# First weights of the next sequence ahead of this one's sums with v, and weights stored whole through DRAM

## The chip, the cores and the metric

One core of a Trainium2 chip. The kernel takes attention inputs and the weights of a channel-mix layer from DRAM and writes one output to DRAM. The metric is the device time of one execution in microseconds; the times given are the median of three runs. TensorE is called PE, VectorE DVE, ScalarE ACT, SyncE SP.

## What is computed

Eight sequences of 576 tokens, 8 heads of 64 channels. 32 packed queries p attend to k and v; then each q attends to the 32 packed values, which serve as keys and as values. The result, 512 channels for each token, goes through a channel mix with a shift by one token. All of it is float32.

```python
def sm_attn(qq, kk, vv):
    s = scale * np.matmul(qq, kk.transpose(0, 1, 3, 2))
    a = np.exp(s - np.max(s, axis=-1, keepdims=True))
    a = a / (np.sum(a, axis=-1, keepdims=True) + 1e-09)
    return np.matmul(a, vv)
p_packed = sm_attn(p, k, v)
out = sm_attn(q, p_packed, p_packed)
...
x_prev = np.concatenate([np.zeros((B, 1, D), dtype=np.float32), x[:, :-1, :]], axis=1)
xk = mu_k * x + (1.0 - mu_k) * x_prev
xr = mu_r * x + (1.0 - mu_r) * x_prev
k = np.maximum(xk @ w_k, 0.0)
v = k * k @ w_v
r = 1.0 / (1.0 + np.exp(-(xr @ w_r)))
return (r * v).astype(np.float32)
```

## The kernel before

The channel mix runs over 9 blocks of 512 tokens. A product of two float32 matrices is made as three matmuls of halves, a high part and the rest (`wk_h`, `wk_l`, and so on), so every 128x512 piece of a product with 128 channels takes three matmuls. Blocks 0 to 2 are done one after the other (`gates`, `keys`, `values`: 48, 96 and 96 matmuls each). Blocks 3 to 8 are done in three pairs, where a pair's products use seven products of sums and differences instead of eight (`products_of`, matmuls at line 1430). They need sums of the weights' blocks, which `chain_of_sums` makes on DVE, splits and sends to DRAM, and differences of the mixed inputs, which `chain_of` makes; the chain of the first pair's keys is called A. Between block 2 and the first pair stand the gates of blocks 3 and 4 (`turned_gates`, lines 1586 to 1588): 96 matmuls, called the seam here with the last of the attention that must be done by then.

Attention of a sequence b goes through these steps. `front`: scores of the packed queries (line 600), weights of both halves of the heads (`weights_of`: maximum at line 667, exponential at line 673). From sequence 2 on the weights are turned by a trip through DRAM (`weights_moved`: a transpose in 32x32 blocks on DVE at line 716, a write `away<-blocks`, four reads `aT<-away` per half). Then, still in `front`, the sums with v (line 622), a division and one transpose on PE. `scores`: second scores (line 749). `back`: softmax over 32 on DVE (lines 765 to 784), a transpose (line 788), products with the packed values (line 796, two bursts for each sequence), copied by ACT to `xt` and stored as `xd`. Scores and products take two slots (`pa`) of two PSUM banks each.

Sequence 0 is split in halves of the heads (`first_side`); its steps stand ahead of the first channel-mix matmul, with dummy matmuls (`spare`) that the planner puts where it reckons PE to be waiting. The weights w_r, w_k, w_v are loaded as pieces of 128x512 (`st`), decoded and split (`convert`, lines 348 to 364).

The order of all of it is made by a planner at build time (class `Flow`): each step is a generator that asks for an engine, a slot or an event, and of those ready the planner takes the one that can start first, with ties by rank. Most numbers at the head of the kernel are ranks. All loads and stores but a few go through SP's queue, in the order in which the planner issues them. Every engine works in order, so the order is fixed once built, and what waits holds up all that is behind it on its engine.

Of the kernel before, what the change touches and what calls it, by code (L numbers as in the profile page):

```python
# [8 lines left out]
F32 = mybir.dt.float32  # L9
# [8 lines left out]
class Flow:  # L18
# [13 lines left out]
    URGENT = 17.786  # L32
# [158 lines left out]
def attn_pack_channel_mix(ctx: ExitStack, tc: tile.TileContext, q, k, v, p, p_first, mu_first, mu_by_channel, w_k, w_v, w_r, out):  # L191
    nc = tc.nc
    B, NPR, P, S = q.shape
    D = P // 2
# [19 lines left out]
    FIRST = 6.558, 12.87, 19.531, 3.995  # L214
    RANK_1, RANK_MIX, RANK_KEYS, RANK_R, RANK_W, RANK_W2, RANK_V, LOADS_1, RANK_SQ, RANK_REST, HOLD_V, HOLD_S = 27.755, 14.838, 10.91, 19.059, 8.25, 30, 30, 23.598, 1.16, -7.23, 0.413, 0.153
    RANK_LATE1 = 0.221
    RANK_LATE2 = 2.192
    RANK_LATE3 = 4.603
    RANK_LATE4 = 0.433
    RANK_LATE5 = 6.623  # L220
    RANK_LATE6 = 7.657
    RANK_LATE13 = 27.996
    RANK_LATE12 = 15.041
# [37 lines left out]
    def reached():  # L261
# [12 lines left out]
    BUFS = dict(kq=8, vt=2, xin=0, pt=1, a0=1, a1=1, aT=1, pm=2, e=4, a2=1, xt=5, tmp=4, xk=NC, sq=NF, sig=4,  # L274
                pa=2, both=1, m=4, n=4, staged=4, ex=3, pair=0, ring=0, store=4, twin=0)
# [11 lines left out]
    RANK_B, RANK_TURN, RANK_BACK, RANK_OUT, RANK_L = 0.2, 1.444, 0.355, 8, 6.94  # L287
    CASTS = 3
    RANK_SUMS = dict(k=28.195, v=34.766, r=31.397)
    CHAINS = dict(A=(1.411, 44.286), B=(11.166, 24.664), RB=(5.884, 12.059), C=(14.13, 14.447), RC=(0.2, 0.2))  # L290
# [9 lines left out]
    for tag, n, size in (  # L300
        ("xk", NC, 2 * TB), ("sq", NF, 2 * TB), ("tmp", 4, WP), ("sig", 4, DM), ("kq", 8, S),
        ("a2", 1, S), ("ex", 3, TB), ("e", 4, S), ("aT", 1, 5 * P), ("vt", 2, NPR * 5 * D),
    ):
        for j in range(n):
            sb.tile([P, size], F32, name=tag, tag=f"{tag}{j}")
    for j, size in enumerate((S, 5 * P)):
        sb.tile([P, size], F32, name="a", tag=f"a{j}")
# [19 lines left out]
    def convert(w, hi, lo, c, o, n, event, first=None):  # L327
# [36 lines left out]
        nc.vector.tensor_tensor(lo[:, c, o:o + n], m.bitcast(F32), hi[:, c, o:o + n].bitcast(F32), op=ALU.subtract)  # L364
        flow.give("tmp", sm)
        flow.set(event)
# [3 lines left out]
    def rank(b, n=0):  # L370

        return (10 if b == 0 else RANK_1 if b == 1 else RANK_B) + 0.1 * (2 * b + n)

    def lrank(b):
        return LOADS_1 if b == 1 else rank(b) if b < 2 else RANK_L + 0.2 * b
# [16 lines left out]

    def loads(b):
        flow.spawn(packed(b), lrank(b) - 0.03)
        for pr in range(NPR):
            flow.spawn(turned(k, "kT", b, pr), lrank(b) - 0.02)
        for h in range(2):
            flow.spawn(values_of(b, h), lrank(b) - 0.01)
        for pr in range(NPR):
            flow.spawn(turned(q, "qT", b, pr), lrank(b))  # L400
        yield from flow.wait(*(("qT", b, pr) for pr in range(NPR)))
# [33 lines left out]
    def first_side(h):  # L435
# [32 lines left out]
        flow.give("a1" if h else "aT", sT)  # L468
# [121 lines left out]

    def front(b):

        yield from flow.wait(("pt", b), *(("kT", b, pr) for pr in range(NPR)))
        slots = yield from two_slots()
# [14 lines left out]
        for h in range(2):  # L609
            flow.spawn(weights_of(b, h, slots[h], s1[h], sm), rank(b) + 0.01 * h)  # L610

        yield from flow.wait(("aT", b, 0))
        slot = yield from flow.take("pa")
# [3 lines left out]
        both = [(*vts.pop((b, h)), *aTs.pop((b, h))) for h in range(2)]  # L617

# [15 lines left out]
        for h, (sv, _, sT, _) in enumerate(both):  # L634
            flow.give("a1" if h else "aT", sT)
            flow.give("vt", sv)
# [6 lines left out]
        sp = yield from flow.take("pm")  # L643
# [8 lines left out]
        nc.tensor.transpose(pT[:, :P], pm.rearrange("p a b -> p (a b)"), ident)  # L652
        ppT = sb.tile([P, P], F32, name="ppT", tag="ppT")
# [8 lines left out]
    def weights_of(b, h, slot, s1, sm):  # L662
# [7 lines left out]
        sa = yield from flow.take(f"a{h}")  # L670
        a = tile_([P, S], F32, "a", h)
# [6 lines left out]
        if b >= MOVED:  # L678
            yield from weights_moved(b, h, sa, a)
            return  # L680
# [7 lines left out]
        if h:  # L688

            sT, aT = sa, tile_([P, 5, P], F32, "a", 1, "aT")  # L690
        else:
            flow.give("a0", sa)
            sT = yield from flow.take("aT")
            aT = tile_([P, 5, P], F32, "aT", sT)
# [15 lines left out]
    def weights_moved(b, h, sa, a):  # L710

        space = "e"
        se = yield from flow.take(space)
# [3 lines left out]
        if h:  # L717

            sT, aT = sa, tile_([P, NPR, 5, NP], F32, "a", 1, "aT")
        else:  # L720
            flow.give("a0", sa)
            sT = yield from flow.take("aT")
            aT = tile_([P, NPR, 5, NP], F32, "aT", sT)
        away = dram.tile([P, NTB, NP], F32, name="away", tag=f"away{h}")
# [15 lines left out]
    def scores(b, sp, pm, ppT, left):  # L740

        yield from flow.wait(*(("qT", b, pr) for pr in range(NPR)))
        slots = yield from two_slots()
# [1088 lines left out]
```

## Time and profile before

| | |
|---|---|
| median of 3 runs | 561.11 us (558.93 to 563.09) |
| profiled execution | 559.48 us |
| its span, first to last instruction | 557.5 us |
| mean granted clock of PE | 0.993 |
| PE busy | 543.8 us, 98% of the span |
| DVE busy | 463.4 us, 83% |
| ACT busy | 388.3 us, 70% |
| transfers | 119.69 MB, 215 GB/s over the span |

The profile shows one execution. A matmul's row gives its start and its duration; matmuls overlap, so the distance between starts is shorter than a duration. What stands in brackets behind a row of the timeline is the idle time before it and what ended it. A window's row gives, after its length, the busy time and the instructions of each engine, then the granted clock, the share of time in which the 16 transfer engines were busy, and GB/s.

### The profile page before, as it was taken

What the parts mean: (1) busy time and instruction counts of PE and PEld (TensorE: products, weight loads), DVE (VectorE), ACT (ScalarE), POOL (GpSimd) and SP (SyncE); (2) the same over time, 40 slices, a digit from 0 to 9 for tenths busy, and PEclk for the clock granted to TensorE, in tenths of its full rate; (3) what the DMA queues carried; (4) which work ended last, traced back from release to release, by engine and by line L of the source; (5) the groups of instructions that cost most, each with busy time, mean ns of one, the idle gap of its engine ahead of it and who ended that gap; (6) DMA issues with size and microseconds to landing.
All of it is one profiled execution on the core that took longest, in us unless ns stands there. A gap on an engine that the chain in (4) does not pass through costs nothing.

```text
span 557.5 us, 10174 instructions
## 1 busy us (share of the span) xinstructions
PE 543.8 (98%) x3571; PEld 421.6 (76%) x3571; DVE 463.4 (83%) x888; ACT 388.3 (70%) x745; POOL 2.8 (1%) x27
## 2 busy tenths in 40 slices
PE   8999999999999999996999999999999999999997
PEld 7956677777776777774888788888888888878885
DVE  1785888989889979999885897957999894799863
ACT  3689897558556777656878775489886748897550
POOL 1000000000000000000000000000000000000000
PEclk9999999999999999997999999999999999999999
DMA  8986956589798998766567814819462681934242
GB/s 278 406 312 245 314 179 210 200 299 320 254 309 249 350 314 268 213 200 200 185 213 229 260 51 148 266 35 287 129 218 78 210 265 33 284 122 152 66 143 94
DMA packets 86930, 119.69 MB, mean 215 GB/s; under 512 B 9440, under 2 KB 58080, under 8 KB 86880
## 3 DMA queue, kind: packets, MB, share of 16 engines
q1 hardware_dynamic: 85600, 117.67, 64.6%
q10 hardware_dynamic: 1280, 1.38, 0.7%
q8 instruction: 28, 0.46, 0.3%
q14 instruction: 22, 0.18, 0.1%
HBM read 87.29 MB, written 31.73 MB: 213 GB/s over the span
## 4 chain that ended last, share of the span: by engine, by line
PE 71%; DVE 11%; DMA 9%; ACT 7%; issue 1%; SPq 0%; DVEq 0%; ACTq 0%
PE ph L1430 44%; PE ph L999 4%; PE ph L1000 4%; PE ph L1001 4%; DMA xin<-xd 3%; PE pa L796 1%; PE pr L1586 1%; PE pr L1587 1%; PE pvo L1099 1%; DMA kT<-in_k 1%; PE pr L1588 1%; PE pr L1070 1%; PE pa L622 1%; DMA qT<-in_q 1%; PE pvo L1100 1%
## 5 line engine op out<-in xcount | busy, mean ns | idle before, releaser
L1430 PE MATMUL ph<-vT,ring 128*128 128x512 f32 x270 | 66.1, 392 | 0.0
L1430 PEld LDWEIGHTS ph<-vT,ring 128*128 128x128 f32 x270 | 50.7, 188 | 11.1
L1430 PE MATMUL ph<-vB,wv_h 128*128 128x512 f32 x140 | 43.7, 394 | 0.8 <-DMA wv_h<-sum 0.8
L1430 PE MATMUL ph<-vT,wv_h 128*128 128x512 f32 x140 | 43.5, 392 | 0.0
L971 DVE SCALAR_TENSOR_TENSOR chain<-xin,mus,chain 128x320 f32<-128x320 f32 (+6 forms) x72 | 35.1, 513 | 7.2 <-ACT chain L967 6.8
L1099 PE MATMUL pvo<-wv_h,sq 128*128 128x512 f32 x96 | 39.3, 409 | 0.0
L999 PE MATMUL ph<-xk,wk_h 128*128 128x512 f32 x96 | 39.1, 408 | 0.0
L1482 ACT COPY ph<-ph 128x512 f32<-128x512 f32 x44 | 25.4, 576 | 19.6 <-PE ph L1430 19.5
L1000 PE MATMUL ph<-xk,wk_h 128*128 128x512 f32 x96 | 37.5, 391 | 0.0
L1100 PE MATMUL pvo<-wv_l,sq 128*128 128x512 f32 x96 | 37.5, 391 | 0.0
L967 ACT ACTIVATE chain<-xin,mus 128x320 f32<-128x320 f32 (+6 forms) x72 | 36.0, 526 | 2.1 <-DMA xin<-xd 2.0
L1101 PE MATMUL pvo<-wv_h,sq 128*128 128x512 f32 x96 | 37.4, 390 | 0.0
L1001 PE MATMUL ph<-xk,wk_l 128*128 128x512 f32 x96 | 37.3, 389 | 0.0
L1118 ACT CAST vT<-c 128x512 fp32r<-128x512 f32 x40 | 24.5, 618 | 15.8 <-PE ph L1430 14.5
L1124 DVE TENSOR_TENSOR c<-c 128x512 f32<-128x512 f32 x48 | 31.9, 691 | 0.1
L1430 PEld LDWEIGHTS ph<-vB,wv_h 128*128 128x128 f32 x140 | 26.2, 188 | 6.8 <-DMA wv_h<-sum 1.1
L1430 PEld LDWEIGHTS ph<-vT,wv_h 128*128 128x128 f32 x140 | 26.2, 188 | 5.8 <-ACT ph L1482 0.3
L1120 DVE TENSOR_TENSOR vT<-c,vT 128x512 fp32r<-128x512 f32 x40 | 26.7, 693 | 1.8 <-ACT vT L1118 1.7
L1124 DVE TENSOR_TENSOR chain<-chain 128x512 f32<-128x512 f32 x40 | 27.3, 690 | 0.5
L1430 PE MATMUL ph<-vB,wv_l 128*128 128x512 f32 x70 | 27.6, 394 | 0.0
L1120 DVE TENSOR_TENSOR vT<-chain,vT 128x512 fp32r<-128x512 f32 x32 | 21.7, 690 | 6.8 <-ACT vT L1118 6.6
L1430 PE MATMUL ph<-vT,wv_l 128*128 128x512 f32 x70 | 27.3, 391 | 0.0
(203 smaller groups left out, 1393.5 us busy)
## 6 DMA issues: line engine op xcount, KB each, us to landing
ring<-sum SPq DMA_DIRECT2D x56, 256.0 KB, 4.1
sum<-sw SPq DMA_DIRECT2D x40, 256.0 KB, 3.8
kT<-in_k SPq DMA_DIRECT2D x32, 288.0 KB, 5.1
qT<-in_q SPq DMA_DIRECT2D x32, 288.0 KB, 5.8
vt<-in_v SPq DMA_DIRECT2D x32, 256.0 KB, 4.6
out<-sig SPq DMA_DIRECT2D x32, 256.0 KB, 2.4
xd<-xt SPq DMA_DIRECT2D x14, 577.0 KB, 4.4
wv_h<-sum SPq DMA_DIRECT2D x28, 256.0 KB, 4.0
```

Of the source, the lines that this page charges most:

```text
L967: nc.scalar.mul(x32[:, o:o + n], x[:, 1:], mus[:, j, c:c + 1])
L971: nc.vector.scalar_tensor_tensor(x32[:, o:o + n], x[:, :n], mus[:, j + 1, c:c + 1], x32[:, o:o + n], op0=ALU.mult, op1=ALU.add,)
L999: nc.tensor.matmul(ph, wk_h[:, c, fs], xh, start=(c == 0), stop=False)
L1000: nc.tensor.matmul(ph, wk_h[:, c, fs], xl, start=False, stop=False)
L1001: nc.tensor.matmul(ph, wk_l[:, c, fs], xh, start=False, stop=(c == NC - 1))
L1099: nc.tensor.matmul(pv[t], sh, wv_h[:, f, :], start=(n == 0), stop=False)
L1100: nc.tensor.matmul(pv[t], sh, wv_l[:, f, :], start=False, stop=False)
L1101: nc.tensor.matmul(pv[t], sl, wv_h[:, f, :], start=False, stop=(n == NF - 1))
L1120: nc.vector.tensor_tensor(lo, x32, hi.bitcast(F32), op=ALU.subtract)
L1124: nc.vector.tensor_tensor(out, x, y, op=op)
L1430: nc.tensor.matmul(bank[2], w, x, start=(not more and step == k == 0), stop=(step == 2 and k == count - 1), skip_group_check=True,)
L1482: nc.scalar.copy(bank[2], base)
```

## The change

Five things are changed, and with them most of the planner's numbers.

1. `front` is cut in two. `front` now makes the scores and weights of sequence b, and a new generator `middles` runs the sums with v (`middle`), so scores and weights of b+1 can stand ahead of the sums of b; b may go no further ahead than the sums of b-2. Loads of k and p of b+1 are spawned with those of b.
2. From sequence 2 on the exponential is written over the scores in PSUM, and the slot is given back after the transpose on DVE. There are 4 buffers aT where there were three others; k and q have 7 buffers instead of 8.
3. Twelve decoded pieces of the weights, the second half of w_k and all of w_v, are stored whole in DRAM (`stored_whole`). `chain_of_sums` loads halves of them (`begin`, `arrives`) where it added `hi` and `lo` before. The other half of w_k and w_r are still added.
4. Only 8 of the 20 pieces of weights are decoded with ACT's first pass; the other 12 get two operations on DVE. Five of eight squares' casts are on ACT, where it was three.
5. The first loads are in another order, and chain A starts after the last load for the mix of gates.

Counted in the two orders: on PE 66 dummies before the first channel-mix matmul become 51; between a sequence's first scores and its sums with v stand 87, 72, 66, 75, 69 and 72 channel-mix matmuls for sequences 2 to 7 before, and 90, 87, 84, 75, 66 and 96 after; between the last second scores and the last burst of line 796 stand 57 before and 96 after; that burst stands 87 matmuls ahead of the first paired product before, 72 after. On DVE there are 890 instructions before and 872 after, on SP 504 and 540.

```diff
...
-    RANK_B, RANK_TURN, RANK_BACK, RANK_OUT, RANK_L = 0.2, 1.444, 0.355, 8, 6.94
-    CASTS = 3
+    RANK_B, RANK_TURN, RANK_BACK, RANK_OUT, RANK_L = 4.771, 1.444, 3.152, 2.969, 32.407
+    CASTS = 5
+    WHOLE = dict(wk=512, wv=0)
...
+        flow.set(event)
+        if event[0] in WHOLE and event[2] >= WHOLE[event[0]]:
+            flow.spawn(stored_whole(event, sm, m.bitcast(F32)), flow.now.rank)
+        else:
+            flow.give("tmp", sm)
...
+    def stored_whole(event, sm, m):
+        kept = dram.tile([P, WP], F32, name="whole", tag="whole%s%d%d" % event)
+        yield from reached()
+        yield from load(kept, m, 0.46, 0.65)
         flow.give("tmp", sm)
-        flow.set(event)
+        wholes[event] = kept
+        flow.set(("whole", *event))
...
         yield from flow.wait(("pt", b), *(("kT", b, pr) for pr in range(NPR)))
+        if b > 2:
+            yield from flow.wait(("summed", b - 2))
+        if b >= MOVED:
+            one = yield from flow.take("e")
+            two = yield from flow.take("e")
+            ahead[b] = [one, two]
         slots = yield from two_slots()
...
+        sms[b] = sm
+        flow.set(("fronted", b))
+
+    def middle(b):
 
         yield from flow.wait(("aT", b, 0))
...
+        out = s1[:, :, :HS]
+        if b < MOVED:
+            sa = yield from flow.take("e")
+            a = tile_([P, S], F32, "e", sa, "a")
+            out = a.rearrange("p (a s) -> p a s", a=2)
         yield act(S + 320, table="exp")
         nc.scalar.activation(
-            a.rearrange("p (a s) -> p a s", a=2), s1[:, :, :HS],
-            AF.Exp, bias=nmx, scale=scale, accum_out=sm[:, h:h + 1],
+            out, s1[:, :, :HS], AF.Exp, bias=nmx, scale=scale, accum_out=sm[:, h:h + 1],
         )
+        if b >= MOVED:
+            yield from weights_moved(b, h, slot, out)
+            return
         flow.give("pa", slot)
...
-        nc.vector.transpose(blocks, a.rearrange("p (k t) -> p k t", t=32))
...
+        nc.vector.transpose(
+            blocks.rearrange("p (a k) t -> p a k t", a=2), a.rearrange("p a (k t) -> p a k t", t=32)
+        )
+        flow.give("pa", slot)
...
+    def arrives(out, src, key):
+        yield from reached()
+        yield from load(out, src, 0.46, 0.33)
+        flow.set(("part", *key))
...
                 def whole(out, a, b):
...
+                    row, col = place(a, b)
+                    if (kind, at, k, a, b) in begun:
+                        yield from flow.wait(("part", kind, at, k, a, b))
+                        return
                     views = (w[:, row, col:col + HD].bitcast(F32) for w in (wh, wl))
                     yield from step(out, *views, ALU.add)
...
+        if i == PAIRS[0]:
+            yield from flow.wait(("fetched", i + 1, NC - 1, 2))
...
+    def middles():
         for b in range(1, B):
             flow.now.rank = rank(b)
-            yield from front(b)
+            yield from middle(b)
```

Three places in the orders. First SP's first loads. Before:

```order
L247 DMA kT<-in_k 128x576 x2
L247 DMA vt<-in_v 128x512 x2
L247 DMA vt<-in_v 64x256
L247 DMA kT<-in_k 128x576 x2
L247 DMA st<-in_moe_w_r 128x1024
L247 DMA vt<-in_v 128x512 x2
L247 DMA vt<-in_v 64x256
L247 DMA st<-in_moe_w_r 128x1024
L247 DMA qT<-in_q 128x576 x4
L247 DMA st<-in_moe_w_r 128x1024 x2
```

After:

```order
L247 DMA kT<-in_k 128x576 x4
L247 DMA st<-in_moe_w_r 128x1024
L247 DMA vt<-in_v 128x512 x2
L247 DMA vt<-in_v 64x256
L247 DMA qT<-in_q 128x576 x2
L247 DMA vt<-in_v 128x512 x2
L247 DMA vt<-in_v 64x256
L247 DMA st<-in_moe_w_r 128x1024 x2
L247 DMA qT<-in_q 128x576 x2
L247 DMA st<-in_moe_w_r 128x1024
```

All four k stand first, q of the first half ahead of v of the second, and three pieces of w_r instead of two ahead of the last q.

Then PE's list for sequence 0, from the first half's sums with v to the second half's second scores (line 465, now 485: sums; 499, now 519: second scores; `spare`: dummies). Before:

```order
L465 MATMUL pv<-vt,aT 32x64 x20
L686 MATMUL pa<-ident,a 128x128 x4
L687 MATMUL pa<-ident,a 64x128
L486 MATMUL pT<-ident,pm 128x128
L1758 MATMUL spare<-ident 128x128 x3
L465 MATMUL pv<-vt,aT 32x64 x20
L499 MATMUL pa<-both,qT 128x64 x10
L486 MATMUL pT<-ident,pm 128x128
L1758 MATMUL spare<-ident 128x128 x2
L499 MATMUL pa<-both,qT 128x64 x10
L1758 MATMUL spare<-ident 128x128 x26
```

After:

```order
L485 MATMUL pv<-vt,aT 32x64 x20
L724 MATMUL pa<-ident,a 128x128 x4
L725 MATMUL pa<-ident,a 64x128
L506 MATMUL pT<-ident,pm 128x128
L1831 MATMUL spare<-ident 128x128 x2
L519 MATMUL pa<-both,qT 128x64 x10
L485 MATMUL pv<-vt,aT 32x64 x20
L1831 MATMUL spare<-ident 128x128 x3
L506 MATMUL pT<-ident,pm 128x128
L1831 MATMUL spare<-ident 128x128 x6
L519 MATMUL pa<-both,qT 128x64 x10
L1831 MATMUL spare<-ident 128x128 x4
```

The first half's second scores moved ahead of the second half's sums, and the 26 dummies behind the second scores are 4, with others further on.

Last DVE's list up to the last transpose back of sequence 7 (`e`, `m`: its softmax; `x`, `xr`: the mix for the gates; `sw`: sums of weights; `sig<-pvo`: outputs of block 2). Before:

```order
L788 STREAM_TRANSPOSE a_3323<-e 128x576
L778 TENSOR_REDUCE m_3297<-e 128x18
L982 TENSOR_TENSOR xr<-x_3306,xr 128x512
L971 SCALAR_TENSOR_TENSOR chain<-xin,mus,chain 128x192
L971 SCALAR_TENSOR_TENSOR chain<-xin,mus,chain 128x320
L780 TENSOR_SCALAR m_3297<-m_3297 128x18
L782 RECIPROCAL m_3297<-m_3297 128x18
L784 TENSOR_TENSOR e<-e,m_3297 128x576
L788 STREAM_TRANSPOSE a_3404<-e 128x576
```

After:

```order
L1147 TENSOR_TENSOR sig<-pvo,sig 128x512 x2
L1008 SCALAR_TENSOR_TENSOR x_3327<-xin,mus,x_3327 128x192
L1008 SCALAR_TENSOR_TENSOR x_3327<-xin,mus,x_3327 128x320
L1008 SCALAR_TENSOR_TENSOR x_3303<-xin,mus,x_3303 128x256
L1147 TENSOR_TENSOR sig<-pvo,sig 128x512 x2
L1019 TENSOR_TENSOR xr<-x_3327,xr 128x512
L1008 SCALAR_TENSOR_TENSOR x_3303<-xin,mus,x_3303 128x256
L1318 TENSOR_TENSOR sw<-sw 128x256
L820 TENSOR_TENSOR e<-e,m_3180 128x576
L1019 TENSOR_TENSOR xr<-x_3303,xr 128x512
L1300 TENSOR_TENSOR sw<-sw 128x256
L825 STREAM_TRANSPOSE a_3404<-e 128x576
```

Chain A's pieces are gone from here, and sums of weights (lines 1300 and 1318) stand between the steps of the softmax. From the first transpose of sequence 7's second scores to this last one there are 33 instructions before and 49 after. Three of the five at line 1300 wait for a transfer.

## Rows read from the trace of the kernel before

**Rows 1.** The page: busy us, share of the span, instructions.
```profile
PE 543.8 (98%) x3571; PEld 421.6 (76%) x3571; DVE 463.4 (83%) x888; ACT 388.3 (70%) x745; POOL 2.8 (1%) x27
```
**Rows 2.** Windows, five stretches: busy of each engine, clock, transfer share, GB/s.
```profile
0.00:34.22 34.22, 32.74 (x306) 27.88 (x307) 19.74 (x41) 19.09 (x37) 1.57 (x15) 1.00 0.96 346
34.22:44.24 10.02, 8.81 (x41) 4.38 (x40) 7.79 (x13) 8.50 (x18) 0.10 (x1) 1.00 0.53 203
44.24:250.26 206.02, 204.64 (x1922) 149.67 (x1922) 181.78 (x388) 145.10 (x284) 1.12 (x11) 1.00 0.81 265
250.26:262.50 12.24, 7.82 (x49) 4.27 (x48) 11.87 (x25) 7.64 (x17) 0.00 (x0) 0.73 0.58 187
262.50:557.50 295.00, 289.84 (x1258) 235.38 (x1256) 242.21 (x424) 207.96 (x392) 0.00 (x0) 1.00 0.52 166
```
**Rows 3.** Timeline of PE, start: start us, us, line, output and inputs, count.
```profile
14.25 0.90 PE L465 MATMUL pv<-vt,aT 128*32 128x64 f32 x40
...
17.53 2.44 PE L499 MATMUL pa<-both,qT 128*128 128x64 f32 x20
...
20.45 2.44 PE L499 MATMUL pa<-both,qT 128*128 128x64 f32 x20
22.73 6.02 PE L1758 MATMUL spare<-ident 128*128 128x128 f32 x52
```
**Rows 4.** Timeline of PE in the seam.
```profile
253.23 0.40 PE L1588 MATMUL pr<-xr,wr_l 128*128 128x512 f32 x1
254.06 0.74 PE L796 MATMUL pa<-a,pm 32*64 32x288 f32 x16 [0.44 <-DVE a L788]
258.15 1.27 PE L796 MATMUL pa<-a,pm 32*64 32x288 f32 x16 [3.34 <-DVE a L788]
259.47 0.79 PE L1586 MATMUL pr<-xr,wr_h 128*128 128x512 f32 x1
```
**Rows 5.** Timeline of DVE: sequence 7's second scores and its two transposes back.
```profile
239.61 0.78 DVE L765 STREAM_TRANSPOSE e<-pa 128x576 f32<-128x576 f32 x1
...
253.15 0.77 DVE L788 STREAM_TRANSPOSE a<-e 128x576 f32<-128x576 f32 x1
...
257.23 0.78 DVE L788 STREAM_TRANSPOSE a<-e 128x576 f32<-128x576 f32 x1
```
**Rows 6.** Windows: the interleaved part, its middle, and the stretch of rows 5.
```profile
60.00:250.00 190.00, 188.99 (x1740) 138.48 (x1725) 171.99 (x369) 129.28 (x253) 1.12 (x11) 1.00 0.81 263
120.00:220.00 100.00, 99.23 (x983) 71.54 (x972) 88.05 (x194) 65.29 (x128) 0.81 (x8) 1.00 0.91 297
239.61:258.01 18.40, 14.17 (x73) 10.41 (x71) 17.55 (x35) 9.71 (x20) 0.00 (x0) 0.94 0.65 203
```
**Rows 7.** Groups by line, DVE: busy us, mean ns, idle before and releaser.
```profile
L353 DVE SCALAR_TENSOR_TENSOR m<-m,st 128x512 uint32<-128x512 uint32 x20 | 13.2, 685 | 4.0 <-ACT m L350 3.8
L1252 DVE TENSOR_TENSOR sw<-wv_h,wv_l 128x256 f32<-128x256 f32 x16 | 6.4, 414 | 0.0
L1022 DVE CAST sq<-r 128x512 fp32r<-128x512 f32 x15 | 6.3, 422 | 1.8 <-PE pvo L1101 0.8 <-ACT r L1014 0.4
```
**Rows 8.** Waits: who waited for whom, us in total, times, longest us.
```profile
PE pa L796 <- DVE a L788: 4.7, 4, 3.3
PE ph L1430 <- DMA wv_h<-sum: 0.8, 1, 0.8
ACT x L967 <- DMA xin<-xd: 8.5, 5, 3.6
```
**Rows 9.** Timeline of SP: write and reads of sequence 2's weights.
```profile
72.29 1.05 SPq L247 DMA_DIRECT2D away<-blocks  x2
75.06 3.65 SPq L247 DMA_DIRECT2D aT<-away  x8
```
**Rows 10.** Timeline of PE: sums with v of sequence 2.
```profile
85.18 1.37 PE L622 MATMUL pa<-vt,aT 128*32 128x64 f32 x80
```
**Rows 11.** The page, transfers by line: count, KB each, us to landing.
```profile
sum<-sw SPq DMA_DIRECT2D x40, 256.0 KB, 3.8
```

More of the change, by code (lines that the diff above doesn't have):

```diff
@@ L391, in first_loads, with first_half @@
             flow.spawn(values_of(0, h), FIRST_V[h])
+    def first_half(b, rank):
+        flow.spawn(packed(b), rank - 0.01)
+        for pr in range(NPR):
+            flow.spawn(turned(k, "kT", b, pr), rank)
     def loads(b):
-        flow.spawn(packed(b), lrank(b) - 0.03)
-        for pr in range(NPR):
-            flow.spawn(turned(k, "kT", b, pr), lrank(b) - 0.02)
+        if b <= MOVED:
+            first_half(b, lrank(b) - 0.02)
         for h in range(2):
             flow.spawn(values_of(b, h), lrank(b) - 0.01)
+        if MOVED <= b < B - 1:
+            first_half(b + 1, lrank(b) - 0.005)
         for pr in range(NPR):
@@ L589, in two_slots @@
         return first, second
+    ahead, sms = {}, {}
     def front(b):
         yield from flow.wait(("pt", b), *(("kT", b, pr) for pr in range(NPR)))
+        if b > 2:
[4 more added lines that the diff above has]
+            ahead[b] = [one, two]
         slots = yield from two_slots()
@@ L609, in front @@
         for h in range(2):
-            flow.spawn(weights_of(b, h, slots[h], s1[h], sm), rank(b) + 0.01 * h)
+            flow.spawn(weights_of(b, h, slots[h], s1[h], sm), flow.now.rank + 0.01 * h)
+        sms[b] = sm
+        flow.set(("fronted", b))
+    def middle(b):
         yield from flow.wait(("aT", b, 0))
+        sp = yield from flow.take("pm")
         slot = yield from flow.take("pa")
@@ L642, in front @@
         nc.vector.reciprocal(rs, rs)
-        sp = yield from flow.take("pm")
+        flow.set(("summed", b))
         pm = tile_([P, 2, D], F32, "pm", sp)
@@ L652, in front @@
         nc.tensor.transpose(pT[:, :P], pm.rearrange("p a b -> p (a b)"), ident)
+        if b > 1:
+            yield from flow.wait(("s2", b - 1, 1))
         ppT = sb.tile([P, P], F32, name="ppT", tag="ppT")
@@ L687, in weights_of @@
         nc.tensor.transpose(tp[:S - NQ, NQ:NQ + P], a[:, NQ:], ident)
[L688 to L694, printed above, removed]
+        flow.give("e", sa)
+        sT = yield from flow.take("aT")
+        aT = tile_([P, 5, P], F32, "aT", sT)
         main, left = (aT[:, :4, :], tp[:, :NQ].rearrange("p (a b) -> p a b", b=P)), (aT[:S - NQ, 4, :], tp[:S - NQ, NQ:NQ + P])
@@ L742, in scores @@
         yield from flow.wait(*(("qT", b, pr) for pr in range(NPR)))
+        one = yield from flow.take("e")
+        two = yield from flow.take("e")
+        ses = one, two
         slots = yield from two_slots()
@@ L757, in scores, with back @@
         for hf in range(2):
-            flow.spawn(back(b, hf, sp, pm, slots[hf], s2[hf], left), rank(b, hf) + (RANK_BACK if b > 1 else -1))
-    def back(b, hf, sp, pm, slot, s2, left):
-        se = yield from flow.take("e")
+            flow.spawn(back(b, hf, ses[hf], sp, pm, slots[hf], s2[hf], left), rank(b, hf) + (RANK_BACK if b > 1 else -1))
+    def back(b, hf, se, sp, pm, slot, s2, left):
         e = tile_([P, NTB, 32], F32, "e", se)
@@ L768, in back @@
         flow.give("pa", slot)
+        if b > 1:
+            yield from flow.wait(("scaled", b - 1, hf))
         m2 = sb.tile([P, NTB + 2], F32, name="m2", tag=f"m2{hf}")[:, :NTB]
@@ L1290, in chain_of_sums @@
                 yield from kept(3, x)
+                yield from begin(x, 1, 0)
                 yield from step(y, y, z)
@@ L1715, in fronts @@
         yield from flow.wait(*(("mixed", h, tag) for h in range(2) for tag in ("xr", "xk")))
+        flow.spawn(middles(), flow.now.rank)
+        for b in range(1, B):
+            flow.now.rank = rank(b) + (RANK_AHEAD if b > 1 else 0.0)
+            yield from front(b)
+    def middles():
         for b in range(1, B):
             flow.now.rank = rank(b)
-            yield from front(b)
+            yield from middle(b)
     def all_loads():
```

97 lines of the change are left out of this document (53 added, 44 removed).

## The prediction

> **What bounds the kernel now.** I read the page's busy shares first, then the span cut into five stretches, then the PE timeline where a stretch loses time, then what VectorE does there. PE is busy for 543.8 of 557.5 us [rows 1], so PE's own queue is the path that sets the end. A change can win only where PE stands idle, runs dummy matmuls, or runs at the lower clock. The five stretches [rows 2] place these: the start up to the first channel-mix matmul, 34.22 us; 10.02 us to the first scores of sequence 1, with 1.2 idle; 206.02 us of channel mix with seven sequences interleaved, 1.4 idle; a seam of 12.24 us, with 4.4 idle and granted clock 0.73; then 295.00 us of paired products, with 5.2 idle.
>
> The seam is where blocks 0 to 2 are done and the turned gates begin, while the last sequence still has two products with its packed values to make (line 796). PE waits 0.44 and then 3.34 us for VectorE's last transposes, and the first matmul after that takes 0.79 us where one before it took 0.40 [rows 4]. At full clock one follows the other by 0.23 us (289.84 us for 1258 in the last stretch [rows 2]). Sixteen matmuls at 0.23 and two bursts of 0.74 make 5.2 us, so the seam loses 7.0. VectorE is the cause: from the first transpose of sequence 7's second scores to the last transpose back [rows 5] it is busy for 17.55 of 18.40 us [rows 6]. On PE only 57 matmuls (13.1 us) and the first of the bursts (0.74) stand over this. The same method gives a loss of 18.4 + about 1.5 (from the scores' start to VectorE's first transpose of them) - 13.9 = 6.0 us, against 7.0 measured, in which the low clock has its share.
>
> PE busy at 98% could be read as nothing left to win. The Trainium skill says in "Perfetto Trace Analysis", Identifying the Most-Contended Engine, that matmul busy time is a poor measure of how near a kernel is to its limit. This trace agrees: matmuls of 0.79 us in the seam, where the one before the wait took 0.40, count as busy [rows 4], and so do dummy matmuls [rows 3].
>
> **The change, part by part.** *Start.* Before the first channel-mix matmul PE has 66 dummies in its order before and 51 after. Twenty-six of them fill 6.02 us [rows 3], 0.23 each, so 15 fewer shorten PE's own list by 3.5 us. That is won only if what they covered comes earlier. Now the values' matmuls of the first half start at 14.25 right behind dummies, and the second scores of its halves stand at 17.53 and 20.45 behind the other half's work [rows 3]. After the change q for the first half is loaded before the second half's v, and its scores stand ahead of the second half's sums. Against it: a third piece of w_r, 0.5 MB, now precedes the second half's q (4.9 MB in Sync's order to the last q, 4.4 before); at 346 GB/s [rows 2] this is 1.5 us later. That half was not held by q but by PE and ScalarE order, so I take 2.5 us won, between -1.5 and 3.5.
>
> *VectorE's work.* Gone: 24 additions of stored halves (8 of w_k, 16 of w_v), 0.42 each [rows 7], 10.0 us; six casts of squares, 0.42, 2.5 us (they go to ScalarE). Added: 12 shifts of 512 columns where a piece is decoded without ScalarE's first pass. No row shows that operation. The nearest are the cast, 422 ns, with one operand tensor as here, and the decoding step with two, 685 ns [rows 7]; I take 0.42, so 5.0 us added, at most 8.2. VectorE is thus relieved by 7.5 us, at least 4.3; ScalarE loses 12 passes and gains 6 casts and two table loads, hidden since it is busy for 129 of the 190 us from 60 to 250 [rows 6].
>
> *First weights ahead.* Scores and weights of b+1 are made before b's sums with v. Counted in PE's order, a moved sequence has 83 channel-mix matmuls on average from scores to sums, where it had 73.5: 2.2 us more for the round trip through DRAM. Second scores to the products back grow nearly everywhere too. The stretch of 206 us idles 1.4 us, 0.9 of it at line 796 (4.7 in all less 3.78 in the seam [rows 4, 8]). I take 1.0 won, between -1 and 1.4. The exponentials now lie in PSUM until VectorE has transposed them, so the two slots are held longer; PE finds them free again since the scores stand that much further ahead.
>
> *Seam.* On PE 96 matmuls (22.1 us) and one burst now lie from the last second scores to the last product back: 22.8 us. VectorE has 49 instructions in the same piece instead of 33: 11 more of the sums (0.42), 3 more splits and 2 more of the mix. That is 18.4 + 6.3 (means less the overlap of about 0.08 each) to 7.6 (means as they are, a split taken at 0.68 as the decoding step), say 25.3, and 1 us from the scores' start. So VectorE is late by 3.5 and PE's two products and the gates between them lose some 3 us instead of 7.0; no wait is as long as 3.34, and I keep the full clock. That is 4.0 won. Bounds: 7.0 if VectorE finds no waits, 1 if the loads of the whole halves hold it. The chain of differences A, which VectorE had begun ahead of the seam (four pieces of the mix in that stretch), is behind it now. It has 72 matmuls (16.6 us) from the last product to the first that needs it; I charge 0.5 us, at most 2.
>
> *Whole pieces through DRAM.* Twelve stores of 256 KB and 24 loads of 128 KB, 6.3 MB. At the 297 GB/s of 120 to 220 us [rows 6] they take 21 us of the transfer engines, which from 60 to 250 us are free for 19% of 190 us, 36 us [rows 6]. Hidden behind 36 us, they would cost what they exceed it if that cover were gone. But VectorE's waits for them are new: before, the halves were read from SBUF. Loads of x are timed in the same way, and ScalarE waited 8.5 us for them in five waits [rows 8]; 1 us of such waits is in the 3 us of the seam. Sums of w_v end earlier, which should close the wait for them in the paired products, 0.8 us [rows 8].
>
> The sum on the profiled execution: 557.5 - 2.5 - 1.0 - 4.0 - 0.8 + 0.5 = 549.7 us of span. Its own time is 559.48, 1.98 above its span, and the median 561.11 is 1.63 above that: 549.7 + 1.98 + 1.63 = 553.3, say **553**.
>
> **Rivals.** *The loads hold VectorE and the seam only moves.* Of the five additions in VectorE's last stretch three wait for a load of a whole half, and nothing behind them on VectorE, the last transposes included, can pass. For: ScalarE waited 1.7 us each time that a load of x was late [rows 8], and VectorE has no room, 17.55 of 18.40 us busy [rows 6]. Against: such loads are asked for as soon as the buffer is free, several instructions ahead, and on PE the last product stands 39 matmuls further off, 9 us. Price: 3 x 1.7 = 5.1 us, of which 1 is in my sum; the seam's 4.0 are gone, 561.1 - 2.5 - 1.0 - 0.3 = 557.
>
> The Trainium skill ("Perfetto Trace Analysis", DMA Optimizations) says that small transfers, under 2 KB, carry a large overhead for each. The loads of whole halves are 1 KB in each partition, half of the rows in which the pieces are stored, so the rule makes this rival likelier. No run here shows such a load yet.
>
> *The start eats it.* The second half's q comes 1.5 us later, and where dummies stood PE is idle. For: the transfers' share is 0.96 over the first stretch [rows 2], so what is moved up moves something back. Against: from 17.53 to 22.73 PE's list, not q, was in the way [rows 3]. 561.1 + 1.5 - 1.0 - 4.0 - 0.3 = 557.
>
> *Slower: the round trip.* Sync's queue is in order, and stores and loads of whole pieces now stand among the writes and reads of the weights. Before, the writes issue at 72.29, the reads by 78.71, and the sums start at 85.18 [rows 9, 10]. A transfer lands 3.8 us after its issue [rows 11], so some 2.7 us are to spare, and 2.2 more after the change. Beyond 4.9 us of delay each of six sequences stops PE. To lose 1% in spite of the 8 us won the six must lose 13.6 us, 2.3 each: trips 7 us longer than now. Then 561.1 + 6 = 567 and above. For: share 0.91 over 120 to 220 us [rows 6]. Against: 36 us are free from 60 to 250, and by their places in Sync's order only about 1.4 of the 6.3 MB fall between 120 and 220.
>
> **How the numbers follow.** One per cent is 5.6 us, about what this kernel's measurement can tell from no change. Forecast, 60%: 553, its own range 547 (start 3.5, seam 7, the middle 1.4) to 555.5. Loads hold VectorE, 18%: 557. The start eats it, 9%: 557, and these two reach 562 where both come together and the seam's 4 us with them. Slower by the round trip, 13%: 567 or more. Faster 0.60, within 1% 0.27, slower 0.13. The range from 547 to 562 leaves out the slower case and a little on the fast side.
>
> **What would show it.** Right: the first channel-mix matmul at 31 to 33 us; PE's idle time at the seam is under 3 us in all, and the granted clock stays at 1.00 there; PE idle under 2 us between the start and the seam; no idle for sums of w_v near 309 us. Wrong: VectorE idle before additions whose input is a whole piece; PE idle at the sums with v; sequences' k, q or v landing late behind stores of whole pieces; PE idle at the first paired product for chain A.

## The result and the profile after

The changed kernel takes 564.18 us (median of 10 runs, 561.16 to 566.89) where the kernel before takes 559.88 beside it: a ratio of 1.0071, 95% interval 1.0045 to 1.0097. It is slower by 0.7%, within the 1% that the prediction called no change, and 11 us above the forecast, outside the range of 547 to 562. The profiled execution took 563.64 us with a span of 561.7. One run of the experiment e9 was slow (567.72 us, at a lower granted clock) and is left out; all other runs, here and below, are fast ones.

Three starts on PE cut both spans alike: the first channel-mix matmul, the first matmul of the turned gates, the first paired product.

| us | before | after | difference |
|---|---|---|---|
| start to the first channel-mix matmul | 34.22 | 30.50 | -3.7 |
| from there to the turned gates | 216.28 | 230.94 | +14.7 |
| from there to the first paired product | 35.93 | 28.41 | -7.5 |
| rest of the span | 271.07 | 271.85 | +0.8 |

One product of sequence 7 (0.74 us) moved from the third stretch into the second, so 0.7 of these two differences is no loss or gain. The start and the seam won 10.5 us; the stretch between them lost 13.9. The four stretches of the changed kernel as windows (columns as in [rows 2]):

```profile
0.00:30.50 30.50, 28.71 (x276) 23.75 (x276) 19.23 (x40) 16.74 (x34) 1.57 (x15) 1.00 0.97 362
30.50:261.44 230.94, 220.18 (x1979) 156.07 (x1978) 189.92 (x397) 154.31 (x302) 1.22 (x12) 0.99 0.84 278
261.44:289.85 28.41, 28.26 (x137) 22.49 (x135) 21.73 (x50) 19.41 (x42) 0.00 (x0) 1.00 0.84 268
289.85:561.70 271.85, 266.79 (x1152) 215.71 (x1152) 228.09 (x385) 194.74 (x366) 0.00 (x0) 1.00 0.50 158
```

In the second PE now idles 10.8 us, where it idled 2.7 before; the rest of the loss is busy time, part of it at a lower clock, as shown below. The waits that end most of this idle time (us in total, times, longest):

```profile
PE pa L628 <- DMA kT<-in_k: 3.2, 3, 1.7
PE pa L656 <- DMA vt<-in_v: 1.8, 3, 1.4
PE pa L686 <- DVE nmx L705: 1.4, 1, 1.4
PE pa L628 <- ACT xt L856: 0.9, 1, 0.9
PE pa L890 <- DVE xr L903: 0.9, 1, 0.9
PE pa L628 <- ACT xt L932: 0.6, 1, 0.6
PE pa L686 <- DVE pm L680: 0.5, 1, 0.5
```

Neither of PE's waits in [rows 8] is among them. Five us are for k and v landing late. The worst place is the sums with v of sequence 3, in the timeline of PE; those of sequence 2 stand above them:

```profile
94.31 1.37 PE L656 MATMUL pa<-vt,aT 128*32 128x64 f32 x80
95.61 0.50 PE L1136 MATMUL pvo<-wv_h,sq 128*128 128x512 f32 x1
...
110.46 0.43 PE L656 MATMUL pa<-vt,aT 128*32 128x64 f32 x16
111.07 0.43 PE L656 MATMUL pa<-vt,aT 128*32 128x64 f32 x16 [0.18 <-DMA vt<-in_v]
112.94 0.43 PE L656 MATMUL pa<-vt,aT 128*32 128x64 f32 x16 [1.44 <-DMA vt<-in_v]
113.53 1.05 PE L656 MATMUL pa<-vt,aT 128*32 128x64 f32 x32 [0.15 <-DMA vt<-in_v]
114.51 0.79 PE L1107 MATMUL pr<-wr_h,xr 128*128 128x512 f32 x1
115.10 0.63 PE L1108 MATMUL pr<-wr_l,xr 128*128 128x512 f32 x1
```

From the first of these sums to the next matmul of the mix it is 4.05 us, where sequence 2 took 1.30; 1.8 of that is waiting. The matmuls behind them take 0.79 and 0.63 us, not 0.39: the granted clock is 0.50, the lower of its two levels (1.2 GHz), from 114.51 to 117.00 us, and those six starts take 2.6 us instead of 1.4. The two buffers of v came free at 95.7, when the sums of sequence 2 (94.31) ended. Sync's timeline from there:

```profile
96.33 7.42 SPq L247 DMA_DIRECT2D aT<-away  x8
103.85 1.10 SPq L247 DMA_DIRECT2D whole<-m  x1
104.99 1.88 SPq L247 DMA_DIRECT2D sw<-whole  x4
106.97 2.98 SPq L247 DMA_DIRECT2D vt<-in_v  x6
```

The load of v stands behind eight reads of weights, a store of a whole piece and four loads of halves, and is issued 11.3 us after its buffer was free. The transfer engines were all but full, too, where k and v landed late: their busy share was 1.05 from 66 to 68 us, 0.94 from 110 to 117 and 1.01 from 203 to 208. PE's sums of sequences 2 and 3 now lie 54 channel-mix matmuls apart, where the closest two lay 90 apart before. Other engines wait for the new transfers as well: VectorE for loaded halves, ScalarE for a buffer from which a piece is still being stored.

```profile
DVE sw L1300 <- DMA sw<-whole: 5.4, 4, 2.4
ACT r L1048 <- DMA whole<-m: 4.8, 1, 4.8
ACT x L971 <- DMA whole<-m: 3.3, 2, 2.7
```

At the seam the two last products of sequence 7 no longer wait. VectorE is busy all the time before the second, and just in time:

```profile
259.28 0.74 PE L833 MATMUL pa<-a,pm 32*64 32x288 f32 x16
266.98 0.74 PE L833 MATMUL pa<-a,pm 32*64 32x288 f32 x16
```
```profile
242.10:266.98 24.88, 24.88 (x162) 18.72 (x161) 24.85 (x56) 15.48 (x33) 0.10 (x1) 1.00 0.87 296
```

### The profile page after: what moved, and what is told of

It reads as the page before. It is cut to its first block, busy times and chain, and to the rows that moved or that the text cites. A ratio compares the mean times of both kernels' runs of the same rounds, so it can differ in the third digit from the quotient of the medians.

```text
span 561.7 us, 10098 instructions
## 1 busy us (share of the span) xinstructions
PE 543.9 (97%) x3541; PEld 418.0 (74%) x3541; DVE 459.0 (82%) x870; ACT 385.2 (69%) x741; POOL 2.8 (0%) x27
## 4 chain that ended last, share of the span: by engine, by line
PE 59%; DMA 13%; DVE 12%; ACT 10%; SPq 3%; issue 2%; ACTq 0%; DVEq 0%
PE ph L1497 42%; DMA xin<-xd 4%; SPq L247 3%; DMA sw<-whole 2%; DMA vt<-in_v 2%; PE pvo L1136 1%; DMA xd<-xt 1%; PE pr L1653 1%; PE spare L1831 1%; PE pvo L1137 1%; PE pr L1654 1%; PE pvo L1138 1%; PE pr L1655 1%; DMA sum<-sw 1%; DMA whole<-m 1%
## 5 line engine op out<-in xcount | busy, mean ns | idle before, releaser
L1008 DVE SCALAR_TENSOR_TENSOR chain<-xin,mus,chain 128x320 f32<-128x320 f32 (+7 forms) x72 | 34.8, 509 | 6.8 <-ACT chain L1004 6.8
```

The lines of the kernel that those rows point to most:

```text
L1008: nc.vector.scalar_tensor_tensor(x32[:, o:o + n], x[:, :n], mus[:, j + 1, c:c + 1], x32[:, o:o + n], op0=ALU.mult, op1=ALU.add,)
```

## Experiments

Most runs keep the changed kernel's planned order, instruction for instruction, and take out or move one thing, since a new plan moves everything (see the last group); e14 does this with the kernel before, and e9 plans it anew. The marks are those above, from each profiled execution; the ratio is to the kernel before, run beside it.

| run | median us | ratio, 95% interval | first mix | to gates | to paired | rest |
|---|---|---|---|---|---|---|
| before | 559.88 | 1 | 34.22 | 216.28 | 35.93 | 271.07 |
| changed | 564.18 | 1.0071 (1.0045-1.0097) | 30.50 | 230.94 | 28.41 | 271.85 |
| e1, three sets of loads gone | 560.58 | 0.9996 (0.9965-1.0027) | 31.07 | 229.75 | 28.30 | 270.18 |
| e2, whole pieces gone | 553.56 | 0.9877 (0.9825-0.9928) | 30.98 | 221.22 | 28.09 | 271.41 |
| e5, slivers | 559.62 | 0.9978 (0.9951-1.0006) | 30.95 | 226.78 | 28.14 | 270.43 |
| e6, issued by GpSimd | 563.22 | 1.0056 (1.0023-1.0088) | 31.03 | 229.49 | 28.13 | 271.55 |
| e7, issued by ScalarE | 563.46 | 1.0056 (1.0025-1.0088) | 30.93 | 233.14 | 28.32 | 270.11 |
| e8, stores gone | 560.55 | 0.9995 (0.9965-1.0025) | 31.11 | 226.91 | 28.60 | 271.58 |
| e13, loads gone | 559.46 | 0.9980 (0.9954-1.0007) | 31.43 | 227.21 | 28.09 | 271.17 |
| e10, added on VectorE | 560.00 | 0.9976 (0.9961-0.9991) | 31.80 | 226.74 | 28.96 | 271.00 |
| e15, added on GpSimd | 557.18 | 0.9945 (0.9918-0.9971) | 31.09 | 224.14 | 28.31 | 270.46 |
| e14, before less 24 additions | 559.26 | 0.9982 (0.9953-1.0010) | 34.26 | 216.42 | 35.78 | 272.94 |
| e9, before, new first loads | 560.28 | 0.9987 (0.9961-1.0014) | 33.17 | 215.15 | 39.03 | 269.65 |

Prices below are differences of these medians. The runs stood beside the kernel before at four times, when its own median was 559.95 to 561.05, and e2 has only four runs. By the ratios the whole pieces cost 10.9 us instead of 10.6, the stores 4.3 instead of 3.6, and VectorE's additions (e10) 5.5 instead of 6.4; so about a microsecond of each price is open.

### What costs the middle: e1 and e2

e1 skips the loads of k of sequences 2 and 7 and v of sequence 3; e2 skips all stores and loads of whole pieces.

```diff
-        yield from load(kept, m, 0.46, 0.65)
+        yield from load(None, m, 0.46, 0.65)      # e2: the planned time passes, nothing is issued
...
-        yield from load(out, src, 0.46, 0.33)
+        yield from load(None, src, 0.46, 0.33)
```

> The changed kernel, with every instruction in the same order, but without three sets of loads: k of sequences 2 and 7 and v of sequence 3. PE reads part of w_k in SBUF in their place, so scores and sums of these sequences are of other numbers; the work is the same. In the changed kernel PE stands 1.7, 0.7, 0.9, 1.4 and some shorter times before these operands, and runs on at the lower clock after the one at 112.9 us; set against undisturbed bursts that is 2.35 + 2.9 + 2.9 + 2.0 = 10.2 us. Theory 'late landings': the middle is lost because these loads land late, and most of the 10.2 us come back: about 554 us, 552 to 557. Theory 'next wait': VectorE and ScalarE are as late behind them, and PE waits for these instead: 561 or more. Theory 'traffic': the 2.9 MB dropped relieve the other transfers too, so that the waits for copies by ScalarE (0.9 and 0.5 us) change as well.

> The changed kernel, with every instruction in the same order, but without the 12 stores of whole pieces and the 24 loads of halves of them; the sums of weights then read tiles filled with zeros once, so the paired products are of other numbers. Theory 'traffic': these 6.3 MB and their 36 places in Sync's queue are what makes k and v late; PE's waits for k and v (5 us, and the low clock behind one of them) go: about 553 us. Theory 'buffers': k and v are late since their buffers come free late (seven instead of eight for k and q, sums with v moved behind the next sequence's weights). Then only the v of sequence 3, with a store and four loads of 3 us in all right ahead of it in the queue, comes earlier; k of sequences 2 and 7 stay late: 558 to 561 us. Neither: 563 or more, as the changed kernel.

Without its late operands (e1) the kernel wins 3.6 us, not 10: PE's waits for VectorE rise in their place (from 3.4 to 7.8 us between 30 and 265). That is nearer to "next wait". Without the whole pieces (e2) it wins 10.6, nearly all in the stretch to the gates, and PE waits for loads for 0.5 us there. In Sync's timeline of e2 v of sequence 3 is issued at 100.53, right behind the reads. That is 6.4 us earlier, and 7.1 instead of 11.3 us after its buffers came free:

```profile
93.77 6.66 SPq L248 DMA_DIRECT2D aT<-away  x8
100.53 3.15 SPq L248 DMA_DIRECT2D vt<-in_v  x6
```

So the whole pieces cause most of the loss in the middle, and late k and v are only the part of it that PE shows.

### Which part of it: e8, e13, e5, e6, e7

e8 leaves out the stores, e13 the loads, e5 moves a sixteenth of the bytes, e6 and e7 issue the 36 transfers from another engine (`nc.gpsimd` or `nc.scalar` in place of `nc.sync`, at the same place of the order).

> The changed kernel, same order, without the 12 stores of whole pieces (3.1 MB); the 24 loads of halves stay, and read parts of k in DRAM, so the paired products are of other numbers. It parts the 10.6 us into those of the stores and those of the loads. Theory 'queue': the stores wait in Sync's queue for VectorE (7.2 us of waits between 40 and 115 us in the changed kernel) ahead of k of sequence 2 and v of sequence 3: most of the 10.6 is theirs, 555 to 558 us. Theory 'VectorE': it is the loads, 561 to 564. Theory 'bytes': half and half, 558 to 560.

> The changed kernel, same order, without the 24 loads of halves (3.1 MB); the 12 stores of whole pieces stay, and the sums' tiles hold zeros at first, so the paired products are of other numbers. Without the stores alone it was 560.6 (3.6 less than the changed kernel), without both 553.6 (10.6 less). Theory 'parts add up': the loads carry the other 7: 557 us. Theory 'either is enough to hold up k, v and VectorE': 560 to 562, and the two parts fall short of the whole.

> The changed kernel, every instruction and transfer in the same order and queue, but each store of a whole piece carries 32 of its 512 columns and each load of a half 16 of 256, so 6.3 MB become 0.4 MB. The rest of the sums' tiles is zero, so the paired products are of other numbers. Dropping these 36 transfers outright gave 553.6 us where the changed kernel has 564.2, so they cost 10.6. Theory 'queue': they cost their places in Sync's queue, where each waits for what it reads or writes and holds the loads of k and v behind it; bytes matter little: 561 to 565 us. Theory 'bytes': the 6.3 MB keep the transfer engines from the loads of k and v: 553 to 556. Theory 'VectorE': the additions wait for loads of halves (5.4 us of waits in the changed kernel), and all that follows on VectorE is late; smaller loads land sooner, but by little: 559 to 563, with these waits above 3 us.

> The changed kernel, every instruction in the same planned order, but the 12 stores of whole pieces and the 24 loads of halves are issued by GpSimd instead of Sync. All bytes move as before; Sync's queue has the order that it has without them. Theory 'queue': PE's waits for k and v fall from 5.0 to about 1 us, and the time to 553 to 557. Theory 'bytes': the waits stay, 562 to 566. Theory 'VectorE': 560 to 564, with VectorE's waits for halves as they are or longer.

> As the kernel with GpSimd as issuer, but with ScalarE. ScalarE spends time on 36 more issues, and waits where the piece or the buffer is not ready, so its own queue is held: theory 'queue': 555 to 560, since part of what Sync's queue wins is lost on ScalarE; theory 'bytes': 563 to 568.

No single theory holds. Stores carry 3.6 us and loads 4.7; with 8.3 of 10.6 the parts nearly add up. With the queue as it is and hardly any bytes 4.6 come back. With Sync's queue freed and all bytes kept 1.0 comes back (e6), which the intervals do not tell from nothing. But e6 changes more than the queue: issued by GpSimd, the loads of halves land later (median us in the last column; first the changed kernel, then e6).

```profile
sw<-whole SPq DMA_DIRECT2D x24, 128.0 KB, 3.8
sw<-whole POOLq DMA_DIRECT2D x24, 128.0 KB, 5.9
```

e6 had won 4.9 us up to matmul 660 of the mix and lost most of it at the first of the two last products. VectorE came late there, and not for a half: it had waited for ScalarE, and ScalarE for a load of x.

```profile
251.78 0.56 ACT L1005 ACTIVATE x<-xin,mus 128x320 f32<-128x320 f32 x1 [2.42 <-DMA xin<-xd]
252.38 0.55 DVE L1009 SCALAR_TENSOR_TENSOR x<-xin,mus,x 128x320 f32<-128x320 f32 x1 [2.57 <-ACT x L1005]
256.79 1.23 PE L834 MATMUL pa<-a,pm 32*64 32x288 f32 x16 [2.31 <-DVE a L826]
```

So the rival "the loads hold VectorE and the seam only moves" is right that the seam can open again, but no run shows a load of a half as what opens it; in the changed kernel VectorE's four waits for halves end at 145.86, 148.43, 209.36 and 225.70 us, ahead of the second scores of sequence 7. What is not told apart is how much of the 10.6 is held buffers (ScalarE's 8.1 us), VectorE's waits (5.4 us) and the queue: each run changes more than one of them.

### VectorE's additions and the seam: e10, e14, e15

e10 takes the stores and loads out and adds the halves on VectorE where it would have waited; e15 adds them on GpSimd where the load would have been issued. e14 is the kernel before without 24 additions.

```diff
-        yield from load(out, src, 0.46, 0.33)
+        nc.gpsimd.tensor_tensor(out, hi, lo, op=ALU.add)   # e15
+        yield from load(None, src, 0.46, 0.33)
```

> The changed kernel in the same planned order, but the 24 halves that it loads are added on VectorE from the two parts in SBUF, as the kernel before does, at the place where it would wait for the load; the 12 stores and 24 loads are gone. VectorE has 24 x 0.42 = 10.0 us more work than in the run without stores and loads (553.6 us). Theory 'traffic costs more than VectorE's additions': 554 to 558. Theory 'VectorE's relief is what closed the seam': the seam opens again by some 5 us and the middle waits more for VectorE: 559 to 564.

> The kernel before, same order, without 24 of VectorE's additions (8 of halves of w_k, 16 of w_v: those that the change takes away); the sums' tiles hold zeros at first, so the paired products are of other numbers. VectorE has 10.0 us less to do, nearly all of it before the turned gates. Theory 'VectorE is the bound up to the seam': the 7 us lost in the seam go, and the wait for the sums of w_v too (0.8): 552 to 555 us. Theory 'order': the seam stays, since its two last products stand right behind each other with VectorE's 33 instructions ahead of them: 557 to 560.

> The changed kernel in the same order, but the 24 halves are added by GpSimd from SBUF at the place where their load was issued; no stores and no loads of whole pieces. Nothing is left out: all the work of the changed kernel, without the way through DRAM. No row shows what an addition takes on GpSimd. Theory 'the way through DRAM': near the run without stores and loads, 553 to 556 us, faster than the kernel before. Theory 'GpSimd in the way': VectorE waits for GpSimd's additions, or both slow each other, as little or less won than with the additions on VectorE (560.0): 560 or more.

e10: 24 additions of 0.42 us cost 6.4 us against e2, 5.5 in the stretch to the gates and 0.9 behind it. The way through DRAM cost 10.6: it is 4.2 dearer than what it replaces. About half of e10's loss lies at the seam, whose first product stands ahead of the gates' mark: against e2 it is 3.5 us behind at matmul 710 of the mix and 7.2 at 732. PE waits there for VectorE's transpose, which ends at 255.45. The bracket names ScalarE, but the product does not read that result, and it starts 0.14 us behind the transpose, as both products of the kernel before do [rows 4, 5]. The granted clock is 0.72 from 258 to 262 us.

```profile
254.67 0.78 DVE L826 STREAM_TRANSPOSE a<-e 128x576 f32<-128x576 f32 x1
255.59 0.74 PE L834 MATMUL pa<-a,pm 32*64 32x288 f32 x16 [1.96 <-ACT x L1005]
```

e14: in the kernel before the same additions cost nothing that can be measured; the seam stands as it was, to the hundredth:

```profile
254.05 0.74 PE L796 MATMUL pa<-a,pm 32*64 32x288 f32 x16 [0.44 <-DVE a L788]
258.14 1.27 PE L796 MATMUL pa<-a,pm 32*64 32x288 f32 x16 [3.34 <-DVE a L788]
```

So in the old order VectorE's relief does not close the seam. The new order does, with the two last products 30 matmuls apart and 66 and 96 behind the second scores, but only about half of it alone: with the additions back on VectorE (e10) some 3.7 of the 7.0 us stay lost. e15 computes everything and is faster than both kernels, 0.9945 of the time before. GpSimd's additions are slow but off the path (busy us, mean ns):

```profile
L1294 POOL TENSOR_TENSOR sw<-wv_h,wv_l 128x256 f32<-128x256 f32 x16 | 15.5, 990 | 65.9 <-DVE sw L1321 49.9 <-DVE rs L675 16.0
L1294 POOL TENSOR_TENSOR sw<-wk_h,wk_l 128x256 f32<-128x256 f32 x8 | 7.4, 947 | 63.7 <-DVE wk_l L366 37.7 <-DVE sw L1321 26.0
```

### The start alone: e9

The ranks of the first loads from the changed kernel, `FIRST` and `RANK_LATE1` to `RANK_LATE6`.

```diff
-    FIRST = 6.558, 12.87, 19.531, 3.995
+    FIRST = 14.499, 7.547, 12.422, 11.979
...
```

> The kernel before with the ranks of the first loads alone taken from the changed kernel (FIRST and RANK_LATE1 to RANK_LATE6). 59 dummies instead of 66 stand before the first channel-mix matmul; the first half's second scores stand ahead of the second half's sums, as in the changed kernel; the rest of PE's order is close to the kernel before, with the last two products at 723 and 729 matmuls. The changed kernel's first channel-mix matmul came at 30.50 us instead of 34.22. Theory 'start carries': 3 to 3.7 us come back here too and reach the end, since PE's list sets the end: about 557 us. Theory 'start is given back': later loads of k, v and the weights are late, or the seam waits longer for VectorE, since PE arrives there earlier: 560 to 562.

The start is given back. PE is 2.5 us ahead at matmul 60 and 2.2 at 720, and 0.9 behind at 780; the turned gates wait for ScalarE and VectorE there:

```profile
252.21 0.50 PE L1586 MATMUL pr<-xr,wr_h 128*128 128x512 f32 x1 [1.37 <-ACT xr L980]
255.23 1.27 PE L796 MATMUL pa<-a,pm 32*64 32x288 f32 x16 [1.22 <-DVE a L788]
258.71 0.79 PE L1586 MATMUL pr<-xr,wr_h 128*128 128x512 f32 x1 [2.21 <-ACT xr L980]
```

### Plans made anew: e3, e4, e11, e12

> The changed kernel, where the planner reckons that a transfer lands 4 us after its time on the engines (LANDS = 4.0) instead of 2. The trace of the changed kernel has medians of 3.4 to 5.8 us from issue to landing. PE's order then holds scores and sums back behind more channel-mix matmuls. Theory 'late landings': PE's waits for k and v shrink below 1.5 us in all and the time falls below the kernel before, to 552 to 557. Theory 'next wait': the stretch still loses 10 us or more to VectorE and ScalarE: 561 or more.

> The changed kernel with the rank of the sequences' loads as before (RANK_L = 6.94 instead of 32.407), so that among transfers that are ready together k, q and v go ahead of stores of sums and of whole pieces. Theory 'order in the queue': k and v land in time, PE's waits for them fall from 5.0 to under 2 us, 555 to 559 us. Theory 'buffers': the loads are asked for as soon as a buffer comes free in either kernel and the rank moves little: 562 to 566.

> The changed kernel with WHOLE empty, planned anew: no piece is stored whole, all sums are added from SBUF. The planner then places the last products of sequence 7 at 795 and 804 channel-mix matmuls instead of 714 and 744, so behind the turned gates' beginning, and sums with v at 48, 213, 264, 396, 471, 636 and 678. Theory 'traffic': PE's waits for k and v fall to under 2 us and the time is 553 to 558. Theory 'VectorE': PE waits for VectorE around 700 to 820 matmuls, and chain A is late for the first paired product by several us: 560 to 566.

> The changed kernel with only half of w_k stored whole (4 stores, 8 loads, 2.1 MB), planned anew; w_v is added from SBUF. The stores of w_k issue at 28 to 38 us in the changed kernel, ahead of the stretch in which k of sequence 2 and v of sequence 3 were late. Theory 'traffic': it lies near the kernel without whole pieces, 554 to 559. Theory 'VectorE': 560 to 566, with waits for VectorE at the last products.

They took 583.35, 576.42, 577.36 and 583.80 us, 12 to 20 above the changed kernel, with single waits of 3.3 to 7.6 us at paired products and gates. Nearly all theories missed; only the open bound of "next wait" in e3 (561 or more) held. Each of these four numbers, changed alone, makes the planned kernel slower; that shows nothing on the part that each takes away: e11 and e10 leave out the same transfers and are 17 us apart.

## Why the prediction was wrong, step by step

- **Start, -2.5:** -3.7 at the first channel-mix matmul, in the range. But at matmul 120, with the same attention work done in both, PE is 1.5 us ahead: the start's lead shrinks when k of sequence 2 lands late. That bit of "the start eats it" is real.
- **Middle, -1.0:** +13.9. This is the step that failed, in two terms. First, the whole pieces were costed at nothing here, "hidden behind 36 us" of free transfer time; they cost 10.6 (e2), 9.7 of it here. A mean share of 0.81 says nothing of the moment when one buffer must be refilled (0.94 to 1.05 where k and v came late), and a transfer in the queue also holds buffers and engines (the 8.1 and 5.4 us above). Second, the two slots in PSUM, held longer for the exponentials, were put at nothing too ("PE finds them free again"). With no whole pieces the stretch is still 4.2 us longer than before (221.22 against 216.28, less 0.74), and the largest wait there is for such a slot. In e2 the packed values of sequence 5 were ready at 168.2, but their transpose on PE starts only when VectorE has transposed the first half of sequence 6's exponentials (to 177.75) and so given a slot back; the releaser in the brackets is VectorE's next instruction, whose result this transpose does not read. VectorE had itself waited 2.6 us for ScalarE before that, and ScalarE 5.7 us for a load of x:
```profile
167.94 0.28 DVE L681 TENSOR_TENSOR pm<-pa,rs 128x128 f32<-128x128 f32 x1
176.98 0.77 DVE L751 STREAM_TRANSPOSE blocks<-pa 128x576 f32<-128x576 f32 x1
177.81 0.33 PE L687 MATMUL pa<-ident,pm 128*128 128x128 f32 x1 [1.90 <-DVE nmx L706]
```
  From 178 to 182 us the granted clock is then 0.59: the nine matmuls and the burst behind the transpose take 4.45 us, in the changed kernel 3.26. So this place accounts for about 3 of the 4.2; the rest is not told apart. The changed kernel has the same wait (the 1.4 us at line 686 above).
- **Where the slack was looked for:** the prediction counted matmuls from scores to sums, 83 against 73.5, and found more room for the weights' round trip. That held: no wait for it. It did not count from one sums to the next, which is the time in which v's two buffers must be refilled: 135, 54, 114, 81, 78 and 105 matmuls now, 108, 117, 90, 105, 96 and 96 before. Nor for k with seven buffers, 75 matmuls between the last two scores. Those numbers stood in PE's order.
- **Seam, -4.0:** -6.8. The mechanism was right, the loss left over was put at 3 us and is none. VectorE was reckoned to need 25.3 us for its 49 instructions; from the first transpose of the second scores (243.45) to the end of the last (266.40) it takes 22.95, and PE came to each of the two products some 0.5 us after VectorE's transpose had ended. The clock stays at 1.00, as said. Part of this may be luck, since PE comes late from the middle, with its second scores at 242.08: in e1, e6 and e10 it has them 2.8 to 5.7 us earlier and waits 1.2, 2.3 and 2.0 us at the first product, though in e2, e5, e13 and e15, earlier too, it waits at most 0.4.
- **VectorE's work:** the shift of 512 columns was taken as 0.42 us and takes 0.422. VectorE's busy time over the whole span fell by 4.4 us (463.4 to 459.0), where 7.5 was taken and 4.3 was the least. The 24 additions alone are worth 6.4 us in the new order (e10) and nothing in the old (e14): work taken off an engine wins only where that engine ends the wait.
```profile
L357 DVE TENSOR_SCALAR m<-m 128x512 uint32<-128x512 uint32 x12 | 5.1, 422 | 2.6 <-ACT m L351 2.6
```
- **Sums of w_v, -0.8 and chain A, +0.5:** the wait for the sums is gone; the first paired products wait 0.3 us once, near 302 us. The rest of the span is 0.8 longer all the same.
- **Rivals:** "slower" had 13% and named the weights' trip as what is late; it was k and v, and v of sequence 3 was held in part by what it named as cause, Sync's queue and the whole pieces in it. Three of the signs named for being wrong came: VectorE idle before additions of whole pieces (5.4 us), PE idle at the sums with v (1.8), and k and v landing late. The rule of the Trainium skill on transfers under 2 KB ("Perfetto Trace Analysis", DMA Optimizations) spoke for a price of the loads of halves. The traces agree with the sign: e13 puts these loads at 4.7 us. They do not show that the size of the pieces is the reason: the stores, at twice the size, cost 3.6 with half as many transfers.
- **The range:** its low end, 547, does not come out of the terms named for it: 557.5 - 3.5 - 7.0 - 1.4 - 0.8 and the 3.6 us from span to median make 548.4. It changes nothing here.

## What to carry to other kernels

For each operand with few buffers, and each slot that is held longer, count in the new order the work from its last use to its next first use, and set against it the queue that its load must pass, or the engine that must give the slot back; a mean share of the transfer engines hides that. Work taken off a busy engine is worth what that engine's waits are worth in this order, and nothing elsewhere; if an idle engine can do it in place (GpSimd here, 557.2 us), that beats a way through DRAM. Where a planner sets the order, test a cause with the order held fixed.

## What was not expected of the hardware

An addition of 128x256 takes 0.95 to 0.99 us on GpSimd (e15) and 0.42 on VectorE. PE's wait of 1.44 us at 112.94, between shorter ones, was followed by a granted clock of 0.50 (1.2 GHz) from 114.51 to 117.00 us; its wait of 1.68 us at 67.83 was not, the clock being 1.00 from 67 to 73 us. The writes of weights land in 4.5 us (median) instead of 2.8; without the whole pieces (e2) they still take 4.3, so these are not the reason, which stays open.
